# A recurrence and a feed-forward layer on one core: r loaded packed from chunk 2 on, its columns put in order by GpSimd, and q k^T for pairs of units

## The chip, the core and the metric

The kernel runs on one core of a Trainium2 chip. The core has five engines with a queue of instructions each: TensorE (PE, matrix products, with PEld for its weight loads), VectorE (DVE), ScalarE (ACT), GpSimd (POOL) and SyncE (SP, which issues transfers); transfers run on 16 DMA engines that all queues share. SBUF is the working memory of 128 partitions; PSUM, with eight banks of 128 x 512 fp32, takes the results of TensorE. The metric is the device time of one execution in microseconds (us), the median of several runs.

## What is computed

B = 4 batches, H = 8 heads, S = 768 tokens, D = 48. First a recurrence along the tokens with one decay `w` and one bonus `u` per head and channel, then a layer with a squared ReLU (384 to 2048 to 384) over all 3072 tokens:

```python
state = zeros(B, H, D, D)
for t in range(S):
    cur = einsum('bhd,bhe->bhde', u[None] * k[:, :, t], v[:, :, t])
    y[:, :, t] = einsum('bhd,bhde->bhe', r[:, :, t], state + cur)
    state = w[None, :, :, None] * state + einsum('bhd,bhe->bhde', k[:, :, t], v[:, :, t])
x = y.transpose(0, 2, 1, 3).reshape(B * S, H * D)
h = maximum(x @ moe_w_in, 0)
out = (h * h) @ moe_w_out
```

All inputs and the output are fp32 in HBM.

## The kernel before

The tokens are cut into six chunks of C = 128; a chunk of one batch is a unit, 24 units in all, unit i = (chunk i // 4, batch i % 4). Inside a unit the recurrence is turned into products: r is multiplied by powers of the decay (`wpos`), k by the inverse powers (`wneg`), and the masked product of the two replaces the loop over tokens. A state per batch carries over from chunk to chunk.

The steps of a unit are small functions:

- `load` brings r, k or v of a unit from HBM, token by token: a partition holds one token, 8 heads of 48 numbers. The units 2 to 5 load through GpSimd's queue, all others through SP's.
- `scale` (L296, instruction on L300, VectorE) multiplies r (x = 0) or k (x = 1) by its powers and writes bf16 into a padded buffer `rkw`, 64 columns a head; `NPAD` such buffers are used in turn.
- `turn` with `evict_rk` (units 0 to 5, TensorE and ScalarE) or `turn_dma` (L306, units 6 to 23, one transfer of SP that transposes) puts r and k with their channels on the partitions, in `rkT`: two heads stand on one set of 128 partitions, 64 rows each.
- `rk` (L326, VectorE) multiplies the two for the term with u. `at` (L331) is q k^T: eight matmuls of 64 rows by 128 columns, two of them (the two heads of a set) in the two halves of the array, into two PSUM banks. `mask` (L346, VectorE, twice a unit) takes a bank to bf16 in SBUF and cuts it to the causal triangle.
- `sums` (L351) makes the term with u and the unit's addition to the state, `diag_v` (L368), `state_add`, `state_decay` (VectorE) and `state_cast` (ScalarE) keep the state, `y_mm` (L393) forms y from the masked product, v and the state, `evict_y` (L412) adds the term with u, and `x_turn` with `evict_x` or `x_dma` (L423, a transfer of SP) transposes y.
- `mm1` (L437) is the first layer (one unit at a time, 12 matmuls of 128 columns a step, for the units 0 to 7; two units at a time, 6 matmuls of 256 columns a step, from unit 8 on), `relu` (ScalarE) and `square` (ScalarE or VectorE) its activation, `mm2` (L466, four matmuls of 384 columns a step) the second layer, `evict_o` (ScalarE) and `store` the way out, mostly through GpSimd's queue.
- `weights` loads a quarter of one weight matrix through GpSimd's queue. `fill` (L244) is a matmul on a constant tile whose result nobody reads.

Nothing but the text `SCHEDULE` sets the order. It is a list of words `step:arguments@banks`; the program goes through it once and calls the functions, and each engine does its instructions in the order in which they are called. A number and a star ahead of a word repeat it; the numbers behind @ are the PSUM banks that the step takes. So a step that is moved in the list is moved past all steps of its engine or queue between the two places. `room` says how many buffers each kind of tile has; an instruction that writes into a buffer waits until the earlier use of it is over.

```python
for word in SCHEDULE.split():
    times, _, word = word.rpartition("*")
    word, _, taken = word.partition("@")
    name, *args = word.split(":")
    given[:] = [int(x) for x in taken.split(",") if x]
    for _ in range(int(times or 1)):
        steps[name](*[value(x) for x in args])
```

`at_pair`, which calls `at` for a unit and for the next one, is in the file; the list before does not use it.

Of the kernel before, what the change touches and what calls it, by code (L numbers as in the profile page):

```python
# [17 lines left out]
load:0:kt fill@0 load:0:rt 2*fill load:1:rt 2*fill load:0:vt fill columns 2*fill spread_log@1 load:1:kt load:2:rt  # L18
load:1:vt weights:kt.0:0:I fill power:0 3*fill load:2:kt power:1 scale:0:0 load:9:kt 3*fill scale:0:1 turn:0:0@2
load:3:rt load:6:kt scale:1:0 fill evict_rk:0:0 fill turn:0:1@3 load:2:vt fill evict_rk:0:1 spread_columns@4  # L20
load:3:kt cast_v:0 rk:0 fill scale:2:0 at:0@5,6 copy_columns fill u_columns mask:0:1 turn:1:0@7 mask:0:0
evict_rk:1:0 weights:-:1:I sums:0@1 weights:-:2:I y_mm:0@2 diag_v:0 load:8:kt fill scale:1:1 2*fill load:3:vt fill
evict_y:0 3*fill scale:2:1 turn:1:1@3 weights:-:0:O 3*fill x_turn:0@4 turn:2:0@6 evict_x:0 fill scale:3:0
weights:-:3:I 2*fill evict_rk:1:1 4*fill evict_rk:2:0 fill rk:1 load:4:rt fill at:1@7,5 turn:2:1@2 mask:1:1
turn:3:0@4 load:5:rt evict_rk:2:1 3*fill mask:1:0 mm1:0:1:0@3 evict_rk:3:0 end_columns rk:2 fill relu:0:1:0 fill
scale:3:1 4*fill cast_v:2 fill load:6:rt at:2@6,5 cast_v:1 fill mask:2:1 4*fill turn:3:1@2 mask:2:0 sums:2@4
evict_rk:3:1 fill sums:1@7 load:4:kt diag_v:2 y_mm:1@3 y_mm:2@5 diag_v:1 mm1:0:1:1@6 weights:-:1:O evict_y:1 fill
relu:0:1:1 3*fill evict_y:2 load:4:vt 2*fill x_turn:1@2 state_add:1 evict_x:1 mm1:0:1:2@3 weights:-:2:O state_add:0
fill relu:0:1:2 fill mm1:1:1:0@6 cast_v:3 rk:3 x_turn:2@5 relu:1:1:0 state_add:2 at:3@2,7 evict_x:2 mm1:1:1:1@3
weights:-:3:O mask:3:1 square:0:1:0:1 sums:3@1 square:0:1:2:1 mask:3:0 mm1:2:1:0@6 load:7:kt square:1:1:0:1  # L30
square:0:1:1:0 mm2:0:0@4 state_cast:1 diag_v:3 y_mm:3@5 mm1:2:1:1@7 relu:2:1:0 evict_y:3 load:5:kt mm2:1:0@2
state_add:3 square:2:1:0:1 state_cast:0 x_turn:3@6 fill load:5:vt mm1:0:1:3@5 relu:1:1:1 mm1:2:1:2@1 scale:4:0
relu:2:1:1 mm1:2:1:3@3 evict_x:3 scale:5:0 fill relu:2:1:3 mm1:3:1:0@7 relu:2:1:2 mm1:1:1:3@6 scale:4:1
square:1:1:1:1 turn:4:0@3 relu:1:1:3 fill mm1:3:1:3@1 evict_rk:4:0 square:1:1:3:0 mm2:2:0@6 relu:3:1:0
square:2:1:1:0 relu:0:1:3 turn:4:1@3 fill square:2:1:3:0 mm1:3:1:1@7 evict_rk:4:1 relu:3:1:3 square:0:1:3:0 mm2:1:1
square:3:1:0:1 rk:4 mm2:0:1 relu:3:1:1 turn:5:0@5 square:2:1:2:1 at:4@3,1 state_cast:2 mm2:3:0@7 mask:4:0
square:3:1:1:1 mm2:0:2 mask:4:1 load:7:rt cast_v:4 mm2:2:1 evict_rk:5:0 sums:4@3 y_mm:4@1 diag_v:4 fill mm2:2:2
evict_y:4 mm2:2:3 scale:5:1 mm2:0:3 state_add:4 x_turn:4@5 load:8:rt turn:5:1@0 evict_x:4 scale:6:1 mm1:1:1:2@1
evict_rk:5:1 mm1:4:1:0@3 relu:1:1:2 rk:5 square:3:1:3:0 at:5@5,0 relu:4:1:0 mm1:4:1:1@1 scale:6:0 cast_v:5 mask:5:0
turn_dma:6 mm1:4:1:3@3 relu:4:1:1 mask:5:1 square:4:1:0:1 sums:5@5 mm2:3:1 diag_v:5 square:1:1:2:1 load:6:vt  # L40
square:4:1:1:0 evict_o:0 mm1:4:1:2@1 store:0:POOL scale:7:0 y_mm:5@0 relu:4:1:2 scale:7:1 mm2:1:2 relu:4:1:3
evict_y:5 turn_dma:7 mm2:1:3 state_cast:3 state_decay:4 square:4:1:3:0 x_turn:5@4 mm2:4:0@1 evict_x:5 scale:8:1
load:9:rt state_cast:4 mm2:4:1 state_add:5 load:7:vt evict_o:1 mm1:5:1:3@3 square:4:1:2:1 state_decay:5 load:10:rt
rk:6 mm1:5:1:0@0 relu:5:1:3 scale:9:1 cast_v:6 at:6@4,5 mm1:5:1:1@2 mask:6:1 mm2:4:2 scale:8:0 relu:5:1:1 rk:7
relu:5:1:0 turn_dma:8 mm2:4:3 mask:6:0 state_cast:5 sums:6@3 square:5:1:3:0 mm1:5:1:2@5 square:5:1:1:1 load:8:vt
diag_v:6 y_mm:6@2 relu:5:1:2 mm1:3:1:2@0 evict_y:6 square:5:1:0:1 at:7@4,5 square:5:1:2:1 x_dma:6 mm2:5:0@2 mask:7:1
relu:3:1:2 mm2:5:1 state_add:6 square:3:1:2:1 load:10:kt load:11:rt cast_v:7 mm2:5:2 scale:9:0 mask:7:0 mm2:3:2
turn_dma:9 scale:10:0 sums:7@0 y_mm:7@5 diag_v:7 mm2:5:3 cast_v:8 state_decay:6 evict_y:7 evict_o:4 at:8@3,4
state_cast:6 state_add:7 store:4:POOL mm2:3:3 x_dma:7 rk:8 mm1:6:1:0@1 store:1:POOL scale:10:1 load:9:vt mm1:6:1:1@5
relu:6:1:0 mask:8:1 load:11:kt mm1:6:1:3@0 mask:8:0 relu:6:1:1 square:6:1:0:1 sums:8@1 square:6:1:1:0 mm1:6:1:2@4  # L50
relu:6:1:3 state_add:8 mm2:6:0@5 relu:6:1:2 turn_dma:10 diag_v:8 evict_o:3 y_mm:8@3 square:6:1:2:1 mm2:6:1 evict_y:8
evict_o:5 state_decay:7 at:9@0,4 x_dma:8 rk:9 mm1:7:1:0@1 mask:9:0 mm1:7:1:1@7 square:6:1:3:0 load:10:vt cast_v:9
load:12:rt relu:7:1:0 mask:9:1 sums:9@3 evict_o:2 mm2:6:2 diag_v:9 square:7:1:0:1 store:2:POOL scale:11:0
mm1:7:1:3@2 relu:7:1:1 state_add:9 store:5:POOL y_mm:9@0 relu:7:1:3 mm1:7:1:2@1 evict_y:9 square:7:1:1:1 scale:11:1
at:10@4,6 x_dma:9 relu:7:1:2 state_decay:8 mm2:7:0@7 state_decay:9 square:7:1:2:1 rk:10 mm2:6:3 turn_dma:11
mask:10:1 mm2:7:1 evict_o:6 square:7:1:3:0 store:6:POOL mm2:7:2 cast_v:10 mask:10:0 load:12:kt state_cast:7
load:11:vt store:3:POOL mm2:7:3 scale:12:0 state_cast:8 sums:10@3 y_mm:10@2 diag_v:10 mm1:8:2:0@0 evict_y:10
mm1:8:2:1@1 x_dma:10 mm1:8:2:3@6 relu:8:2:1 state_cast:9 mm1:8:2:6@5 square:8:2:1:0 load:13:rt load:13:kt rk:11
at:11@4,2 relu:8:2:0 scale:12:1 mm1:8:2:4@1 relu:8:2:3 turn_dma:12 square:8:2:0:1 mm1:8:2:2@0 square:8:2:3:0
relu:8:2:4 mask:11:1 mm1:8:2:5@6 relu:8:2:2 load:12:vt mask:11:0 mm2:9:0@1 cast_v:11 load:14:rt square:8:2:4:1  # L60
state_add:10 mm1:8:2:7@2 square:8:2:2:1 sums:11@0 relu:8:2:6 y_mm:11@4 diag_v:11 mm2:8:0@3 relu:8:2:7 evict_y:11
relu:8:2:5 mm2:8:1 state_decay:10 x_dma:11 scale:13:1 square:8:2:5:1 mm2:9:1 scale:13:0 square:8:2:6:1 mm2:9:2
square:8:2:7:0 turn_dma:13 evict_o:7 at:12@5,2 rk:12 mm2:8:2 mask:12:0 load:13:vt cast_v:12 mm2:8:3 mask:12:1
load:14:kt mm2:9:3 load:15:rt sums:12@4 mm1:10:2:0@6 diag_v:12 load:15:kt y_mm:12@7 relu:10:2:0 mm1:10:2:1@5
evict_y:12 state_cast:10 rk:13 mm1:10:2:2@2 x_dma:12 state_add:11 relu:10:2:1 at:13@6,7 evict_o:9 square:10:2:1:0
# [51 lines left out]
def kernel(  # L117
# [13 lines left out]
    C = 128  # L131
# [14 lines left out]
    room = {'ldr': 3,  # L146
            'ldk': 8,
            'ldv': 4,
            'rkw': 4,
            'g': 2,  # L150
            'rkT': 3,
            'vb': 6,
# [405 lines left out]
```

## Time and profile before

| | us |
|---|---|
| median of 3 runs | 178.05 (177.88 to 178.28) |
| the profiled execution | 177.38 |
| its span, from the first to the last instruction | 175.6 |
| TensorE busy | 169.5 |
| VectorE busy | 130.0 |
| ScalarE busy | 128.3 |
| GpSimd busy | 32.6 |
| fills (L245), 68 of them, busy | 14.0 |
| `at` (L337), 192 matmuls, busy | 9.7 |
| loads of r through SP's queue, 20, from issue to landing (median) | 4.4 |
| transposes of `rkw` through SP's queue, 18, from issue to landing (median) | 3.8 |

The span starts at 0 with the first instruction; 1.8 us of the execution lie around it. A line of a group gives the source line, the engine, the operation, the tiles written and read with their shapes, how many there were, the busy time and the mean length of one, then the idle time of the engine ahead of them and what ended it. A matmul's length counts from its start to the end of its last result, so that matmuls that follow each other overlap in the record, and busy times of the lines of TensorE add up to more than the engine's. Slices cut the span into 40 equal parts, with the busy share of each in tenths.

### The profile page before, as it was taken

Reading aid. Unit: us, or ns where it says so; the run is one execution under the profiler, and the core shown is the slowest. Engines: PE = TensorE matmul, PEld = TensorE weight load, DVE = VectorE, ACT = ScalarE, POOL = GpSimd, SP = SyncE. Lnnn points to the kernel's source line nnn. Section 1 sums busy time; section 2 is a strip of 40 time slices with the busy share of each in tenths; the row PEclk is TensorE's granted clock in tenths of the full one; section 3 lists DMA queues with packets and bytes.
Section 4 is the critical chain, followed back from the end, with each engine's and each line's share of the span. In section 5 each row is a group of like instructions: output and inputs, shape, how many; then the busy total and the mean of one; then the engine's idle time right before and its main releaser. Section 6 shows DMA issues by size and latency. Waiting matters only on the chain.

```text
span 175.6 us, 4843 instructions
## 1 busy us (share of the span) xinstructions
PE 169.5 (97%) x1946; PEld 134.0 (76%) x1946; DVE 130.0 (74%) x280; ACT 128.3 (73%) x266; POOL 32.6 (19%) x66
## 2 busy tenths in 40 slices
PE   7999999999999999999999999999999999999990
PEld 3668889868777788787786896886895976879770
DVE  4486897658998999878699989889777598560400
ACT  4616599976889499599396797499497894895930
POOL 8987444000100202200020003000030300000020
PEclk9999999999999999999999999999999999999998
DMA  5999999994797998799899999978999996410023
GB/s 109 197 221 183 218 221 214 232 166 95 156 181 136 235 157 215 175 193 155 168 157 223 182 139 257 197 139 165 191 221 173 204 199 115 82 52 19 0 90 134
DMA packets 93848, 28.83 MB, mean 164 GB/s; under 512 B 89681, under 2 KB 91730, under 8 KB 93826
## 3 DMA queue, kind: packets, MB, share of 16 engines
q1 hardware_dynamic: 89472, 18.88, 62.1%
q0 software_dynamic: 4352, 9.64, 23.1%
q8 instruction: 15, 0.25, 0.6%
q14 instruction: 7, 0.06, 0.1%
q10 hardware_dynamic: 2, 0.00, 0.0%
HBM read 20.45 MB, written 4.72 MB: 143 GB/s over the span
## 4 chain that ended last, share of the span: by engine, by line
PE 94%; ACT 1%; DVE 1%; issue 1%; POOL 0%; ACTq 0%
PE bank L447 37%; PE bank L471 35%; PE bank L245 5%; PE bank L337 4%; PE bank L400 3%; PE bank L362 2%; PE bank L406 2%; PE bank L320 2%; PE bank L486 2%; PE bank L357 1%; PE bank L249 1%; PE bank L431 1%; ACT L190 0%; ACT rkT L324 0%; ACT lnw L209 0%
## 5 line engine op out<-in xcount | busy, mean ns | idle before, releaser
L447 PE MATMUL bank<-xT,w_in_q 128*128 128x128 bf16 (+1 forms) x768 | 70.8, 246 | 0.0
L471 PE MATMUL bank<-w_out_q,g 128*128 128x384 bf16 x368 | 67.4, 326 | 0.0
L447 PEld LDWEIGHTS <-w_in_q 128*128 128x128 bf16 x768 | 64.1, 114 | 2.3
L455 ACT ACTIVATE gr<-bank 128x512 f32<-128x512 f32 x96 | 54.3, 599 | 15.5 <-PE bank L447 14.7
L471 PEld LDWEIGHTS <-g 128*128 128x128 bf16 x368 | 33.7, 98 | 19.4 <-ACT g L462 0.5
L462 ACT ACTIVATE g<-gr 128x512 bf16<-128x512 f32 x60 | 36.2, 636 | 0.5
L505 POOL DMA_DIRECT2D out_dram<-osb x21 | 11.4, 545 | 128.4 <-ACT osb L478 127.9
L349 DVE TENSOR_TENSOR am<-bank,smask 128x512 bf16<-128x512 f32 x48 | 31.7, 686 | 3.2 <-PE bank L337 2.9
L464 DVE TENSOR_TENSOR g<-gr 128x512 bf16<-128x512 f32 x36 | 24.4, 686 | 12.8 <-ACT gr L455 12.8
L391 ACT CAST stb<-st 64x192 bf16<-64x192 f32 x40 | 13.9, 348 | 5.7 <-DVE st L385 5.4
L371 DVE TENSOR_TENSOR dv<-vb,bank 128x384 f32<-128x384 bf16 x24 | 13.2, 552 | 6.3 <-PE bank L362 4.7
L300 DVE TENSOR_TENSOR rkw<-ldr,wpos 128x384 bf16<-128x384 f32 x24 | 13.3, 553 | 3.6 <-ACT wpos L253 2.4
L415 DVE TENSOR_TENSOR yb<-bank,dv 128x384 bf16<-128x384 f32 x24 | 13.3, 556 | 2.7 <-PE bank L406 1.7
L245 PE MATMUL bank<-warm 128*128 128x256 bf16 x68 | 14.0, 335 | 1.2 <-DVE warm L193 1.2
L304 ACT CAST vb<-ldv 128x384 bf16<-128x384 f32 x24 | 12.3, 511 | 3.8 <-DMA ldv<-in_v_dram 3.7
L478 ACT COPY osb<-bank 128x384 f32<-128x384 f32 x23 | 10.9, 477 | 4.9 <-PE bank L471 4.9
L300 DVE TENSOR_TENSOR rkw<-ldk,wneg 128x384 bf16<-128x384 f32 x24 | 13.3, 553 | 0.9 <-DMA ldk<-in_k_dram 0.7
L329 DVE TENSOR_TENSOR rk<-rkT 128x512 bf16<-128x512 bf16 x24 | 10.1, 421 | 4.2 <-ACT rkT L324 2.6
L381 DVE TENSOR_TENSOR st<-bank,st 64x192 f32<-64x192 f32 x32 | 11.3, 352 | 0.9 <-PE bank L362 0.6
L245 PEld LDWEIGHTS <-warm 128*128 128x128 bf16 x68 | 7.2, 116 | 3.9 <-issue 1.3
L337 PE MATMUL bank<-rkT 64*128 64x128 bf16 x192 | 9.7, 222 | 0.0
L337 PEld LDWEIGHTS <-rkT 64*128 64x128 bf16 x192 | 5.5, 95 | 5.2 <-issue 3.2
(61 smaller groups left out, 118.0 us busy)
## 6 DMA issues: line engine op xcount, KB each, us to landing
out_dram<-osb POOLq DMA_DIRECT2D x21, 192.0 KB, 3.7
ldk<-in_k_dram SPq DMA_DIRECT2D x20, 192.0 KB, 4.5
ldr<-in_r_dram SPq DMA_DIRECT2D x20, 192.0 KB, 4.4
ldv<-in_v_dram SPq DMA_DIRECT2D x20, 192.0 KB, 4.0
w_in_q<-in_moe_w_in_dram POOLq DMA_DIRECT2D x4, 384.0 KB, 9.9
w_out_q<-in_moe_w_out_dram POOLq DMA_DIRECT2D x4, 384.0 KB, 11.7
ldr<-in_r_dram POOLq DMA_DIRECT2D x4, 192.0 KB, 10.5
ldk<-in_k_dram POOLq DMA_DIRECT2D x4, 192.0 KB, 9.1
```

The lines of the kernel that those rows point to most:

```text
L245: nc.tensor.matmul(out=bank("fill")[:, :WIDE], lhsT=warm[:, :128], rhs=warm, start=True, stop=True)
L300: nc.vector.tensor_tensor(t["rkw"][:, x, :, :, :D], pair(src), pair(wx), ALU.mult)
L337: nc.tensor.matmul(out=t["at"][o][:, p, :], lhsT=t["rkT"][sl, 1, p, :], rhs=t["rkT"][sl, 0, p, :], start=True, stop=True,)
L349: nc.vector.tensor_tensor(am, t["at"][o], smask.unsqueeze(1).to_broadcast([C, HP, C]), ALU.mult)
L371: nc.vector.tensor_tensor(t["dv"], t["vb"], t["d"].unsqueeze(2).to_broadcast([C, H, D]), ALU.mult)
L391: nc.scalar.copy(stb[b][sl, :, o * D : (o + 1) * D], st32[b][sl])
L415: nc.vector.tensor_tensor(t["yb"], t["y"], t["dv"].rearrange("p h d -> p (h d)"), ALU.add)
L447: nc.tensor.matmul(out=t["h", s][:, a], lhsT=turned, rhs=chunks[c]["xT"][:, n, b : b + m, :], start=(n == 0), stop=(n == NK - 1),)
L455: nc.scalar.activation(t["gr", s], t["h", s], AF.Relu)
L462: nc.scalar.activation(g, x, AF.Square)
L464: nc.vector.tensor_tensor(g, x, x, ALU.mult)
L471: nc.tensor.matmul(out=t["o"], lhsT=chunks[units[i][0]]["g"][:, f, units[i][1], :], rhs=w_out_q[f // 4][:, f % 4, :], start=(f == 0), stop ...
```

## The change

The units of the chunks 0 and 1 stay as they are. For the chunks 2 to 5, r is treated a chunk at a time:

- `load4` loads one batch of a chunk with four tokens on a partition (32 partitions, 8 heads, 4 x 48 numbers in one run), so that four loads fill the 128 partitions with the four batches.
- `scale4` multiplies two of the four token places of all four batches at once by powers of the decay that belong to this layout (`wpos4`, made by `power4` on ScalarE from a copy of the log, `keep_log`), `turn4` transposes them, in two halves each.
- In what comes out, the columns of a unit stand as (place of four, token of 32). `gather` copies them for one unit into the order of the tokens, on GpSimd, into one of three buffers `rTu`.
- k of two neighbouring units is scaled into one buffer (`scale_k`) and transposed by one transfer (`turn_k`).
- `at_pair` makes q k^T of both units one after the other, with four banks taken.

The numbers of loads and of transposing transfers stay (72 and 36), and the matmuls and fills do too. `packed_consts` prepares constants on GpSimd. Numbers of buffers change (`room`, `NPAD` 5), and the whole list is written anew: steps that the change does not name stand elsewhere too.

```diff
-    PAIRED = ()
+    PAIRED = (8, 10, 12, 14, 16, 18, 20, 22)
-    room = {'ldr': 3, ..., 'rkw': 4, 'rk': 3, 'am': 4, 'gr': 6, ...
+    room = {'ldr': 4, ..., 'rkw': 5, 'rk': 2, 'am': 9, 'gr': 8, ...
+            'ldr4': 1, 'rw4': 1, 'r4T': 2, 'kw2': 2, 'kT2': 2, 'rTu': 3}
...
+    def packed_consts():
+        time = const.tile([128, 1], mybir.dt.int32, name="time")
+        for b in range(B):
+            nc.gpsimd.iota(time[b * NP : (b + 1) * NP], pattern=[[0, 1]], base=0, channel_multiplier=J)
+        for j in range(J):
+            nc.gpsimd.tensor_scalar(up4[:, j : j + 1], time, 1.0, float(j - C // 2), ALU.mult, ALU.add)
+        for x in rw4_b + kw2_b:
+            nc.gpsimd.memset(x[:, :, :, :, D:], 0.0)
+    def keep_log():
+        nc.scalar.copy(lnb, spread["log"])
+    def power4(j):
+        nc.scalar.activation(wpos4[:, j].rearrange("p h d -> p (h d)"), lnb, AF.Exp, scale=up4[:, j : j + 1])
+    def load4(c, b):
...
+        nc.sync.dma_start(
+            out=chunks[c]["r4"][b * NP : (b + 1) * NP].rearrange("p h j d -> p h (j d)"),
+            in_=r[b, :, c * C : (c + 1) * C, :].rearrange("h (p j) d -> p h (j d)", j=J),
+        )
+    def scale4(c, n):
...
+        j = slice(2 * n, 2 * n + 2)
+        nc.vector.tensor_tensor(
+            x["rw"][:, j].rearrange("p j a o e -> p j (a o) e")[:, :, :, :D], x["r4"][:, :, j, :].rearrange("p h j d -> p j h d"),
+            wpos4[:, j], ALU.mult,
+        )
+    def turn4(c, n):
...
+        nc.sync.dma_start_transpose(
+            out=x["rT"][:, j].rearrange("p j a c -> p (j a) c"), in_=x["rw"][:, j].rearrange("p j a o e -> p (j a o e)"),
+        )
+    def gather(i):
+        c, b = units[i]
+        x = tiles[i]["rT"] = buffer("rTu", [128, HP, C], BF16)
+        e = nc.gpsimd if ('POOL', 1.0)[0] == "POOL" else nc.vector
+        e.tensor_copy(
+            x.rearrange("p a (q j) -> p a j q", j=J), chunks[c]["rT"][:, :, :, b * NP : (b + 1) * NP].rearrange("p j a q -> p a j q"),
+        )
+    def scale_k(i):
...
+        nc.vector.tensor_tensor(t["kw"][:, :, :, :D], pair(t["kt"]), pair(wneg), ALU.mult)
+    def turn_k(i):
+        x = buffer("kT2", [128, 2, HP, C], BF16)
+        nc.sync.dma_start_transpose(
+            out=x.rearrange("p n a c -> p (n a) c"), in_=pairs[i]["kw"].rearrange("p n a o e -> p (n a o e)"),
+        )
...
     def at(i):
...
-                    out=t["at"][o][:, p, :], lhsT=t["rkT"][sl, 1, p, :], rhs=t["rkT"][sl, 0, p, :],
+                    out=t["at"][o][:, p, :], lhsT=t["kT"][sl, p, :], rhs=t["rT"][sl, p, :],
```

`rk`, `sums` and `y_mm` read the new tiles in the same way. Some places of the list, before and after:

```diff
-load:0:kt fill@0 load:0:rt 2*fill load:1:rt 2*fill load:0:vt fill columns 2*fill spread_log@1 load:1:kt load:2:rt
-load:1:vt weights:kt.0:0:I fill power:0 3*fill load:2:kt power:1 scale:0:0 load:9:kt 3*fill scale:0:1 turn:0:0@2
...
-square:8:2:7:0 turn_dma:13 evict_o:7 at:12@5,2 rk:12 mm2:8:2 mask:12:0 load:13:vt cast_v:12 mm2:8:3 mask:12:1
-load:14:kt mm2:9:3 load:15:rt sums:12@4 mm1:10:2:0@6 diag_v:12 load:15:kt y_mm:12@7 relu:10:2:0 mm1:10:2:1@5
...
+load:1:rt fill@0 load:0:rt 2*fill load:0:kt 2*fill load:0:vt fill columns fill spread_log@1 load:1:kt load:3:rt
+load:1:vt load:2:rt fill power:0 fill weights:rt.1:0:I power:1 scale:0:0 load:6:kt spread_columns@2 scale:0:1
+load:2:kt turn:0:0@3 scale:1:0 turn:0:1@4 evict_rk:0:0 load:3:kt fill evict_rk:0:1 turn:1:0@5 load:2:vt rk:0 fill
...
+x_dma:8 state_decay:8 mm1:7:1:0@2 mask:9:0 relu:7:1:1 evict_o:5 mask:9:1 mm2:6:1 load4:3:1 relu:7:1:0 store:5:POOL
+scale_k:11 mm1:7:1:3@3 square:7:1:1:1 turn_k:10 square:7:1:0:1 sums:9@6 y_mm:9@7 diag_v:9 mm1:7:1:2@5 square:6:1:3:0
+load:10:vt mm2:6:2 relu:7:1:2 evict_y:9 relu:7:1:3 state_add:9 mm2:7:0@1 x_dma:9 square:7:1:2:1 fill square:7:1:3:0
+mm2:7:1 load:11:vt scale4:3:1 mm2:6:3 load:12:kt mm2:7:2 evict_o:6 scale4:3:0 state_cast:8 at_pair:10@2,5,7,3
...
+cast_v:12 gather:14 load:15:kt mm2:9:2 cast_v:13 load:14:kt mm2:9:3 load:14:vt rk:12 at_pair:12@5,7,2,6 evict_o:9
+load4:4:2 sums:12@1 load:15:vt mask:12:1 mm1:10:2:0@3 mask:12:0 mm1:10:2:2@4 relu:10:2:0 load4:4:3 diag_v:12
...
+square:14:2:7:0 mm2:15:0@1 relu:14:2:5 gather:19 diag_v:17 square:14:2:5:1 mm2:14:0@7 evict_y:17 store:12:POOL
+square:14:2:4:1 mm2:14:1 state_add:17 x_dma:17 relu:14:2:6 store:10:POOL at_pair:18@0,6,2,4 rk:18 square:14:2:6:1
```

More of the change, by code (lines that the diff above doesn't have):

```diff
@@ L23 @@
[L23 to L62, printed above, removed]
@@ L298, in scale @@
         t["rkw"] = rkw_b[i % NPAD]
+        t["kw"] = t["rkw"][:, 1]
         src, wx = (t["kt"], wneg) if x else (t["rt"], wpos)
```

201 lines of the change are left out of this document (135 added, 66 removed).

## The prediction

> **What bounds the kernel now.** I read the head of the page (busy times, 40 slices, the chain's share by engine), then the table of ten-microsecond windows, then the timeline of TensorE around one q k^T step, and last the rows for the engines that get new work.
>
> ```profile
> PE 169.5 (97%) x1946; PEld 134.0 (76%) x1946; DVE 130.0 (74%) x280; ACT 128.3 (73%) x266; POOL 32.6 (19%) x66
> PE   7999999999999999999999999999999999999990
> PE 94%; ACT 1%; DVE 1%; issue 1%; POOL 0%; ACTq 0%
> ```
>
> TensorE never rests, and the chain that ended last is TensorE for 94%. So time is gained only where TensorE's own list gets shorter, and lost only where something makes it wait. Busy TensorE is not TensorE at its pace, so I looked at where one group starts and the next one starts:
>
> ```profile
> 64.00 0.81 PE L471 MATMUL bank<-w_out_q,g 128*128 128x384 bf16 x4
> 64.75 0.40 PE L337 MATMUL bank<-rkT 64*128 64x128 bf16 x8
> 65.08 1.53 PE L447 MATMUL bank<-xT,w_in_q 128*128 128x128 bf16 x24
> 69.50 3.42 PE L471 MATMUL bank<-w_out_q,g 128*128 128x384 bf16 x20
> 72.76 0.24 PE L357 MATMUL bank<-uwb,rk 128*128 128x8 bf16 x4
> ```
>
> Columns: start, length, line. Twenty L471 start to start take 72.76 - 69.50 = 3.26, 0.163 each. So the four at 64.00 are through at 64.65, but `at` (L337, two half-height matmuls side by side) starts at 64.75 and the next step at 65.08. One `at` holds TensorE 65.08 - 64.65 = 0.43 us. Its four side-by-side pairs of 128 columns need 4 x 0.056 = 0.22 (0.67 us for the 12 matmuls of 128 columns in the chain of waits). **About 0.21 us of each `at` is the way into and out of the half-height form**, 24 times in the span.
>
> **The change, part by part.**
>
> *Pairs.* From unit 8 sixteen `at` become eight pairs of 16 half-height matmuls in a row: eight ways in and out fewer, 8 x 0.21 = 1.7 us. The other matmuls are the same in number and shape, fills too (68 before and after). If the second half must wait for its own operand, the gain is nothing: the bounds are 0 and 1.7. I take 1.7, since the operand of the second unit is listed well ahead (below).
>
> *Loads of r.* Sixteen loads of 1024 runs of 192 bytes become sixteen of 256 runs of 768 bytes, each into 32 partitions. Queue q1 spends 0.621 x 16 x 175.6 / 89472 = 19.5 ns on a packet of 211 bytes on average, q0 149 ns on one of 2215; 768 bytes lie at an estimated 56 ns. So 16384 x 19.5 - 4096 x 56 = 90 us over 16 engines, 5.7 us of DMA time saved. It buys nothing by itself: no DMA holds the chain. But one chunk's r is now whole only when four loads have landed, and the first half that `scale4` multiplies is then waited for on VectorE with masks and squares queued behind it. Words of the list go to each engine in order; the TensorE steps between two words are the time that the other engine has. From the last load of chunk 3 to its `scale4` these are two narrow mm1 (1.34), `sums` and `y_mm` (0.6), two or three mm2 (1.3 to 1.95): 3.3 to 3.9 us, against 4.4 us to landing for a load of r now and 1.7 for the smallest transfer in the trace. Chunk 2 has 6.4, chunks 4 and 5 have 4.6 and 5.2. A wait of 0 to 1.1 us once; 0.1 at the end, since VectorE has 10% to spare there.
>
> *VectorE.* `scale` of r goes 16 times at 0.553 (8.8 us); `scale4` comes 8 times at 0.95 (0.553 for 384 columns and 0.686 for 512 give 1.04 ns a column, 768 columns), 7.6 us. k is scaled as before. 1.2 us less on an engine that is off the path: nothing.
>
> *SP's queue.* 16 transposes become 8 `turn4` and 8 `turn_k` of the same 1024 columns, so the queue's length (1.2 to 1.9 us each) stays. `turn4` moves ahead of v loads and x transposes; from the second `turn4` of chunk 2 to the first pair stand 8.7 us of TensorE steps, against 3.8 to landing and two gathers.
>
> *GpSimd.* Sixteen gathers of 16 runs of 32, written with a step of 4: new to the trace. The nearest rows:
>
> ```profile
> masks.py:199 POOL TENSOR_SCALAR_AFFINE_SELECT identb<-identb 128x128 bf16<-128x128 bf16 x1 | 0.3, 294 | 0.1
> masks.py:199 POOL TENSOR_SCALAR_AFFINE_SELECT ident<-ident 4x4 f32<-4x4 f32 x1 | 0.2, 185 | 0.1
> masks.py:197 POOL MEMSET ident<- 4x4 f32 x1 | 0.1, 92 | 0.3 <-POOLq L542 0.3
> ```
>
> 124 more columns cost 109 ns, so 512 columns cost 185 + 508 x 0.88 = 0.63 us; that is the lower bound. If each of the 16 runs cost as much as the smallest instruction, 16 x 92 ns = 1.47 us is the upper one. I take 0.63, the row of the same form. 16 x 0.63 = 10 us on an engine that is busy 19%. A gather waits for its transpose and, with three buffers, for the `y_mm` three gathers back; behind it in the queue are stores of the output, for which four output buffers and the copies into them on ScalarE wait. The tightest is that of unit 19: it needs `y_mm` of 17, and three mm2 (1.95 us) later the pair 18/19 comes. Even 1.47 fits: nothing. `packed_consts` (four iota, four small arithmetic, three memsets, some 2.3 us from rows of 0.1 to 0.5) stands ahead of three loads of w_out, hidden in the waits of 1.9, 0.8 and 2.3 us that this queue has there now (on L455, a DMA, L371); 2.3 if they are gone.
>
> *ScalarE.* `keep_log` and four `power4` at 0.58 (row of L253) are 2.9 us in the first 50, where the windows show 15 us idle: nothing, and 2.9 if that cover were gone.
>
> *Masks.* A pair fills four of eight banks, and `y_mm` follows closer: after pair 12/13 come `sums` and two mm1, 1.6 us, where 2.9 stood between; two masks take 1.3. I add 0.3 for these places together (bounds 0 and three times 0.6).
>
> **Sum:** -1.7 + 0.1 + 0.3 = -1.3 us. The profiled execution took 177.38 us (span 175.6), so its like after is 176.1. The median of the runs is 178.05, 0.67 above the profiled one, so I forecast 178.05 - 1.3 = **176.7 us**.
>
> **Rivals.**
>
> *VectorE is held up by the gathers and becomes the bound (slower).* The windows, in columns of start:end, PE, PEld, DVE:
>
> ```profile
> 60.00:70.00 10.00, 10.00 (x170) 8.53 (x168) 9.76 (x22) 8.31 (x17) 1.08 (x2) 1.00 1.02 205
> 70.00:80.00 10.00, 10.00 (x104) 8.23 (x103) 8.18 (x17) 7.74 (x18) 1.08 (x2) 1.00 0.98 191
> 80.00:90.00 10.00, 10.00 (x117) 7.58 (x113) 8.00 (x17) 7.26 (x16) 0.00 (x0) 1.00 0.93 165
> 90.00:100.00 10.00, 9.97 (x107) 7.54 (x106) 9.71 (x23) 7.49 (x17) 1.08 (x2) 1.00 1.09 180
> 100.00:110.00 10.00, 10.00 (x109) 7.75 (x106) 9.19 (x19) 8.77 (x19) 1.63 (x3) 1.00 1.01 202
> ```
>
> VectorE is busy 44.8 of 50 us there, with 0.6 less after. If every gather stops it for its whole length, about eight gathers fit up to (50 - 44.2) / 8 = 0.72 us each; from there VectorE sets the pace and TensorE waits. At 1.05 us, half way between my bounds, it is 8 x 1.05 - 5.8 = 2.6 late; with further gathers in the remaining windows at 7 to 9 of 10 I add 0.4: 178.05 - 1.7 + 3.0 = **179.4**. For it: the two crowded windows. Against it: `scale` takes 548 to 560 ns in all 24 cases, also those beside GpSimd's DMA issues, so no stop shows so far; no GpSimd compute of such length runs beside VectorE in this trace. The Trainium skill, SBUF — State Buffer, section Who interferes with whom, speaks for it: a VectorE instruction with two SBUF inputs and a GpSimd instruction that reads SBUF exclude each other, and the later one waits for the whole of the first. By that rule only squares, `scale`, `rk` and the decay would stop, not masks and what reads a bank; no run here shows it yet.
>
> *The front gives part back.* Ahead of the first transpose stand 9 fills (15 before), ahead of the first mm2 55 (63 before), and the other 13 come later, the last near unit 7's mm2. If the front's data come no sooner, TensorE idles where 8 fills stood and pays them later: 8 x 0.11 = 0.9, **177.6**.
>
> *The clock is released later.* Seven fills from 10.88 take 0.21 us each, nine from 14.09 take 0.12:
>
> ```profile
> 10.15 0.25 PE L357 MATMUL bank<-uwb,rk 128*128 128x8 bf16 x4 [0.35 <-POOL uwb L267]
> 10.88 1.67 PE L245 MATMUL bank<-warm 128*128 128x256 bf16 x7
> 12.35 0.63 PE L320 MATMUL bank<-identb,rkw 128*128 128x128 bf16 x4
> 14.09 1.15 PE L245 MATMUL bank<-warm 128*128 128x256 bf16 x9
> 15.17 0.40 PE L337 MATMUL bank<-rkT 64*128 64x128 bf16 x8
> ```
>
> So TensorE goes at half pace until about 14.0, which is 3.9 us after the last idle piece (ended at 10.15). Fewer fills mean more idle; if one such piece moves the release by 3.9 us, half of it is lost: 178.05 - 1.7 + 1.9 = **178.25**, no change. The same skill's page TensorE: Matmul & The Clock Gate, Part 1, ties the release to free-running windows of about 3.4 us of sustained work; by that figure the loss would be 1.7. The trace agrees in kind (3.9 us without a gap).
>
> *The change does not do what it says:* the second `at` of each pair stands until its own gather is through, so the ways in and out are not saved but waited: 178.05 + 0.1 + 0.3 = **178.45**.
>
> **Numbers.** Forecast 0.50, VectorE 0.26, front 0.12, clock 0.08, no saving 0.04. What can be told from no change here is 0.2%, 0.36 us. Faster takes the forecast but 0.01 and 0.11 of the front: 0.60. Slower is VectorE: 0.26. The rest, 0.14, is the same. The forecast's own range is 175.2 (the front also shortens by its 8 fills, the small waits are not there, and 0.2 for the scatter of the runs: 178.05 - 1.7 - 0.9 - 0.2) to 177.4 (the small waits at half their upper bounds more); with the rivals 175.2 to 180.4, the upper end being VectorE at a gather of about 1.2 us.
>
> **What would show it.** Right: eight L337 groups of 16, each some 0.65 us from the end of the step before to the start of the next; TensorE idle nowhere after 20 us; gathers near 0.63. Wrong: groups that start late after a gather or a mask, `scale` or squares longer than 0.69 beside a gather, a DMA wait of some tenths before `scale4`, fills at 0.21 beyond 14 us.

## The result and the profile after

| | before | after |
|---|---|---|
| median | 178.03 us (177.88 to 178.28, 4 runs) | 183.06 us (182.11 to 184.24, 4 runs) |
| the profiled execution, its span | 177.38, 175.6 | 183.33, 181.6 |
| start of the last matmul in its trace | 170.9 | 176.8 |

The changed kernel is slower: ratio 1.0284, 95% interval 1.0221 to 1.0347. The forecast was 176.7 us with a range up to 180.4. A median here is taken over all runs of a kernel; a ratio is taken to the kernel before, timed beside it, and leaves out runs over 1.5% longer than the kernel's fastest.

First the head of the page of after and its groups on the engines that got new work (columns as in the tables before: busy us, mean ns of one, idle time before them and what ended it). In this kernel L303 is `gather`, L553 `square`, L438 `mask`, L316 `scale_k`, L320 `turn_k`, L426 `at`, L446 `sums`, L536 `mm1`, L560 `mm2`, L513 `x_dma`:

```profile
PE 168.1 (93%) x1946; PEld 133.2 (73%) x1946; DVE 136.7 (75%) x274; ACT 132.0 (73%) x271; POOL 56.8 (31%) x93
PE   6699999999999989999999799796999999999990
PE 32%; DMA 8%; DVE 8%; issue 0%; DVEq 0%; SPq 0%
...
L303 POOL COPY rTu<-r4T 128x512 bf16<-128x512 bf16 x16 | 22.6, 1465 | 57.1 <-DMA r4T<-rw 22.5
L553 DVE TENSOR_TENSOR g<-gr 128x512 bf16<-128x512 f32 x36 | 27.5, 776 | 13.3 <-ACT gr L544 13.1
L438 DVE TENSOR_TENSOR am<-bank,smask 128x512 bf16<-128x512 f32 x48 | 32.0, 685 | 2.6 <-PE bank L426 2.2
L316 DVE TENSOR_TENSOR kw<-ldk,wneg 128x384 bf16<-128x384 f32 x16 | 10.5, 660 | 0.1
```

TensorE, without a gap before, now has slices of 8, 7 and 6 tenths between 60 and 130 us (a slice is 4.5 us). The chain that ended last, followed back to 89.9 us, is now DMA and VectorE for a third of its length, where it was TensorE for 94% of the span. A gather takes 1.38 us at the median, 1.47 in the mean. VectorE has 1.2 us less to do by the change and is busy 6.7 us more: the square of 512 columns went from 686 to 776 ns, the scaling of k from 553 to 660, while the mask, which reads a bank, kept its 685. The waits of TensorE (us in total, times, longest):

```profile
PE bank L426 <- DMA kT<-kw: 2.4, 2, 1.4
PE bank L446 <- DVE rk L418: 1.4, 1, 1.4
...
PE bank L446 <- DVE am L438: 0.7, 1, 0.7
```

A pair in TensorE's timeline (start, length):

```profile
108.49 2.76 PE L560 MATMUL bank<-w_out_q,g 128*128 128x384 bf16 x16
111.19 0.62 PE L426 MATMUL bank<-rTu,kT 64*128 64x128 bf16 x16
111.74 1.47 PE L560 MATMUL bank<-w_out_q,g 128*128 128x384 bf16 x8
```

Sixteen L560 at 0.163 are through at 111.10, the next step starts at 111.74: a pair holds TensorE 0.64 us, where two single `at` held it 2 x 0.43. All eight pairs show it, two of them behind a wait.

**Where the time went.** Both lists of TensorE hold the same matmuls, so I took each matmul's start and subtracted the work listed before it at its own pace, fills left out. The difference between the two traces is then what was lost up to there. It is 0.2 us after the first 5 us of work, about 1.2 at 7, 1.3 at 40 and 5.9 at the end. After 40 us of work the pairs take off 1.6, so the waits that are new there are some 6.2 us: 1.3 at 63 us of the span, 1.1 at 100, 1.5 at 113, 0.3 at 117, 1.6 at 124, 0.4 at 152.

Three of them in the trace. At 63 and at 113 us, VectorE's and then GpSimd's timeline:

```profile
61.54 1.83 DVE L474 TENSOR_TENSOR st<-st,wend_c 128x192 f32<-128x192 f32 x1
63.40 0.69 DVE L438 TENSOR_TENSOR am<-bank,smask 128x512 bf16<-128x512 f32 x1
...
110.78 2.39 DVE L553 TENSOR_TENSOR g<-gr 128x512 bf16<-128x512 f32 x1
```

```profile
62.02 1.39 POOL L303 COPY rTu<-r4T 128x512 bf16<-128x512 bf16 x1
...
111.51 1.34 POOL L303 COPY rTu<-r4T 128x512 bf16<-128x512 bf16 x1
```

The state's decay, 0.35 us at the median, lasts until 63.37, where the gather ends at 63.41. Behind it in VectorE's queue is the mask, and `sums` on TensorE waits for that. The square at 110.78, 0.69 us elsewhere, lasts until 113.17; `rk` comes late behind it, and `sums` waits 1.4 us for `rk`. Both instructions start in the record 0.5 to 0.7 us ahead of the gather, while GpSimd issues a store, and without the gather would have been over by its start: why they were held that early is open (in e9 below, no instruction beside a store's issue is longer). At 100 us it is SP's queue:

```profile
92.47 2.31 SPq L513 DMA_TRANSPOSE xT<-yb  x1
94.83 0.57 SPq L275 DMA_DIRECT2D ldr<-in_r_dram  x1
95.45 0.45 SPq L364 DMA_DIRECT2D ldk<-in_k_dram  x1
96.01 2.25 SPq L320 DMA_TRANSPOSE kT<-kw  x1
```

k of units 14 and 15 is scaled at 94.17. SP issues an x transpose and two loads first, `turn_k` starts 1.8 us later and lands at 101.14, 5.1 us after its start (median 3.3), and the pair stands until then. At 124 it is the same: scaled at 118.29, the x transpose of unit 16 ahead, `turn_k` issued at 120.19 and landed 6.0 us later.

### The profile page after: what moved, and what is told of

It reads as the page before. It is cut to its first block, busy times and chain, and to the rows that moved or that the text cites. A ratio compares the mean times of both kernels' runs of the same rounds, so it can differ in the third digit from the quotient of the medians.

```text
span 181.6 us, 4885 instructions
## 1 busy us (share of the span) xinstructions
PE 168.1 (93%) x1946; PEld 133.2 (73%) x1946; DVE 136.7 (75%) x274; ACT 132.0 (73%) x271; POOL 56.8 (31%) x93
## 5 line engine op out<-in xcount | busy, mean ns | idle before, releaser
L536 PE MATMUL bank<-xT,w_in_q 128*128 128x128 bf16 (+1 forms) x768 | 71.5, 246 | 1.0 <-DMA w_in_q<-in_moe_w_in_dram 0.4
L536 PEld LDWEIGHTS <-w_in_q 128*128 128x128 bf16 x768 | 64.1, 113 | 4.5 <-DMA w_in_q<-in_moe_w_in_dram 0.9
L560 PE MATMUL bank<-w_out_q,g 128*128 128x384 bf16 x368 | 67.3, 326 | 0.0
L560 PEld LDWEIGHTS <-g 128*128 128x128 bf16 x368 | 34.1, 98 | 19.5 <-ACT g L551 0.4
L303 POOL COPY rTu<-r4T 128x512 bf16<-128x512 bf16 x16 | 22.6, 1465 | 57.1 <-DMA r4T<-rw 22.5
L553 DVE TENSOR_TENSOR g<-gr 128x512 bf16<-128x512 f32 x36 | 27.5, 776 | 13.3 <-ACT gr L544 13.1
L551 ACT ACTIVATE g<-gr 128x512 bf16<-128x512 f32 x60 | 36.9, 634 | 0.7
L438 DVE TENSOR_TENSOR am<-bank,smask 128x512 bf16<-128x512 f32 x48 | 32.0, 685 | 2.6 <-PE bank L426 2.2
L331 PE MATMUL bank<-warm 128*128 128x256 bf16 x68 | 15.2, 320 | 1.2 <-DVE warm L200 1.2
L567 ACT COPY osb<-bank 128x384 f32<-128x384 f32 x23 | 10.8, 480 | 5.1 <-PE bank L560 4.9
L413 ACT COPY rkT<-bank 128x512 bf16<-128x512 bf16 x12 | 6.7, 587 | 9.2 <-PE bank L409 9.2
L316 DVE TENSOR_TENSOR kw<-ldk,wneg 128x384 bf16<-128x384 f32 x16 | 10.5, 660 | 0.1
L331 PEld LDWEIGHTS <-warm 128*128 128x128 bf16 x68 | 6.7, 111 | 4.1 <-issue 1.3
L418 DVE TENSOR_TENSOR rk<-rTu,kT 128x512 bf16<-128x512 bf16 x16 | 7.7, 485 | 2.6 <-DMA kT<-kw 2.5
L489 PE MATMUL bank<-vb,am 128*128 128x48 bf16 x192 | 8.8, 183 | 0.0
```

The costliest lines, as they stand in the source:

```text
L303: e.tensor_copy(x.rearrange("p a (q j) -> p a j q", j=J), chunks[c]["rT"][:, :, :, b * NP : (b + 1) * NP].rearrange("p j a q -> p a j q"),)
L331: nc.tensor.matmul(out=bank("fill")[:, :WIDE], lhsT=warm[:, :128], rhs=warm, start=True, stop=True)
L438: nc.vector.tensor_tensor(am, t["at"][o], smask.unsqueeze(1).to_broadcast([C, HP, C]), ALU.mult)
L536: nc.tensor.matmul(out=t["h", s][:, a], lhsT=turned, rhs=chunks[c]["xT"][:, n, b : b + m, :], start=(n == 0), stop=(n == NK - 1),)
L551: nc.scalar.activation(g, x, AF.Square)
L553: nc.vector.tensor_tensor(g, x, x, ALU.mult)
```

## The experiments

Theory A: the gathers stop VectorE wherever it reads two operands from SBUF, and TensorE waits for what is late. Theory B: the k transposes are late by their place in SP's queue. The rivals were that only the gather's latency counts, that the new list loses time by itself, and, later, that the transfers in flight make the transposes late. The expectations call A the port theory.

### Set 1: the gather

**e1_unpacked**: the changed list with its pairs, but r loaded token by token and no gather.

```diff
-        nc.sync.dma_start(out=chunks[c]["r4"][b * NP : (b + 1) * NP]..., in_=r[b, ...].rearrange("h (p j) d -> p h (j d)", j=J))
+        nc.sync.dma_start(out=chunks[c]["r4"][:, b], in_=r[b, :, c * C : (c + 1) * C, :].rearrange("h s d -> s h d"))
...
+        tiles[i]["rT"] = chunks[c]["rT"][:, b]
```

> The same list with pairs, but r of chunks 2 to 5 is loaded token by token again (one batch into a quarter of the tile), multiplied by two instructions of 384 columns where one of 768 stood, and the gather is gone (its units read the transposed tile directly). Port theory (a gather takes GpSimd 1.47 us and stops VectorE's instructions with two SBUF inputs meanwhile, 8.0 us of VectorE in all, which is what TensorE waits for after 60 us): VectorE busy 136.7 - 8.0 - 7.5 + 8.8 = 130, TensorE's waits after 60 us fall from 6.3 to under 1.5, time 183.1 - 5 = 178. Latency theory (only the length of the gather on its own queue): the same, 178. List theory (pairs that take four banks, masks close behind, k transposes late in SP's queue): the waits stay, 181 or more.

185.01 us (183.38 to 186.96), ratio 1.0363 (1.0291 to 1.0435). VectorE went back to 130.3 us busy, with the square at 688 and the scaling of k at 553 ns. That is A's part of the trace. The time did not follow: its TensorE waits 4.1 us for `kT` and 2.2 for `xT`. So A alone does not explain the list; the edit also put 192-byte runs back, so it does not say what the gathers cost. (e9 below has the same list, no gathers either, and packed loads, and took 180.65.)

**e2_gather_act** and **e3_gather_dve**: the gather on ScalarE and on VectorE.

```diff
-        e.tensor_copy(
+        nc.scalar.copy(
...
-        e.tensor_copy(
+        nc.vector.tensor_copy(
```

> The gather is done by ScalarE in the same places of the list, 16 x 0.59 = 9.4 us more on an engine that is busy 132 of 182. Port theory: VectorE falls by 8.0 to 128.7, TensorE's waits after 60 us mostly go, some come back through a later ScalarE: 178.5 to 179.5. Latency theory: the same. List theory: 182 or more.

> The gather is done by VectorE in the same places of the list: 0.42 to 0.69 us each by the rows of 512 columns. Port theory: VectorE gets 6.7 to 11 us of copies in place of 8.0 us of stops, 136 to 140 busy, so TensorE waits much as in the changed kernel: 181.5 to 184. Latency theory: operands are ready 0.8 to 1 us sooner, 178 to 179.5. List theory: 183.

192.89 us (192.01 to 194.04), 1.084 (1.0774 to 1.0905), and 186.26 (184.18 to 188.26), 1.0424 (1.0349 to 1.05). VectorE's stretching is gone in e2 (129.5 us busy), but ScalarE is busy 149.2 us instead of 132.0, a gather taking it 1.35, and that costs more. On VectorE a gather takes 0.75 us and the engine comes to 138.3 us busy, about what the stops make of it on GpSimd (136.7). GpSimd is the least bad place for it in this list.

**e4_gather_twice**: each gather made a second time, into a spare tile.

```diff
+        for y in (gather_spare, x):
```

> Each gather copies twice on GpSimd, the first time into a tile that nobody reads: 2.9 us a unit in place of 1.47. Port theory: the stops double, VectorE 142 to 145 busy, 187 or more. Latency theory: only the gathers with little cover come later (units 9, 19, 16), 184 to 186, VectorE's own time as before. List theory: 183.

192.94 us (191.53 to 194.53), 1.0796 (1.0722 to 1.0869), VectorE 149.0 us busy, 12.3 more for 16 gathers more. Idle time on GpSimd would have hidden them; their stops on VectorE did not stay hidden. This speaks for A, though not alone: TensorE also waited 2.0 us for a gather itself, which is latency.

### Set 2: the k transposes earlier

**e5_unpacked_early** (from e1), **e6_packed_early** (from the changed kernel): from chunk 3 `scale_k` and `turn_k` one to three steps earlier, r loads 6 to 12 us earlier. **e7_packed_early_apart** is e6 with the pairs apart, **e8_packed_early_front** is e6 with the first 30 us in the order of before.

```diff
-... load4:4:1 scale_k:14 sums:13@5 load:16:kt relu:10:2:3 y_mm:13@4 scale_k:15 ... turn_k:14
+... mask:12:0 scale_k:14 ... scale_k:15 turn_k:14 load:15:vt mask:13:0 ... x_dma:12 ... load:16:kt
```

> Unpacked r as in the first experiment (185.01 us), and the order of the work changed in one respect: from chunk 3 the scalings and the transpose of k of each pair stand 1 to 3 us earlier, ahead of the x transpose and of the loads that stood directly before them, and the r loads of chunks 3 to 5 stand 6 to 12 us earlier. Theory 'k transposes late by their place in SP's order': TensorE's waits at the pairs of units 10, 14 and 18 (1.1, 1.6, 1.6 us) go and with them some of the 2.6 us that mm1 waited for x transposes: 178 to 180.5 us. Rival 'the loads token by token and the pair transposes do not fit in the time that is there, wherever they stand': the waits move, 184 to 186 us.

> The changed kernel (183.06 us) with the same new order, r packed and gathered on GpSimd. Theory 'two causes add: k transposes late by their place (1.04 + 1.5 us at the pairs of units 14 and 18), VectorE stopped beside gathers (1.3 + 1.5 + 0.3 us at 63, 113 and 117)': the first goes, the second stays, 180 to 181 us. Rival 'the gather alone': the k waits are only where time is spent that the gathers have already lost, so 182.5 to 183.5 us. Rival 'the list alone': all of the late waits go, 177.5 to 179 us.

> The run before this one with every pair of q k^T groups taken apart by one mm1 or mm2 step. Theory 'a pair saves one way into and out of half-height matmuls, 0.21 us, eight times': 1.7 us more than the run with pairs, 181.7 to 182.7 us if that takes 180.5. Rival 'the ways are hidden in other waits of TensorE': within 0.4 us of the run with pairs.

> The packed kernel in the new order, and its first 30 us (up to the transpose of unit 6) in the order of the kernel before, with the packed constants set in between. Theory 'the front's new order costs 1.0 to 1.3 us (fewer fills, a wait of 1.3 us for the w and u columns and of 0.5 us for w_in)': 179 to 179.8 us if the second run takes 180.5. Rival 'the front lost nothing that counts': within 0.4 us of the second run.

190.63 us (189.32 to 192.46), 193.8 (193.05 to 198.43), 194.22 (193.34 to 195.38) and 193.25 (193.11 to 194.59): all over 10 us above what the theory under test had named (e5 is 4.6 above its rival's range too). In e6 SP stood 16.7 us in total before `turn_k`, waiting for the scaled k, and the x transposes behind it in the same queue came late: TensorE waited 5.1 us for `xT` in four places, 2.6 for one `kT`. A transpose put ahead of its operand on an in-order queue holds everything behind it. e7 and e8 differ from e6 by less than its runs scatter; on an order that is held up by SP they say nothing on pairs or front. (In e8 one bank of the second product is written again before it is copied out; its work is that of e6.)

### Set 3: one cause at a time

**e9_no_gather**: the changed kernel, its list and loads, without gathers (a unit reads other tokens' columns, so the output is another; e12, e13, e14 and e17 do the same).

```diff
-        x = tiles[i]["rT"] = buffer("rTu", [128, HP, C], BF16)
...
+        tiles[i]["rT"] = chunks[c]["rT"][:, b]
```

> The changed kernel with its own order and the 16 gathers of GpSimd left out: a unit reads 128 columns of the transposed r as they lie, which are other tokens' (the output is another). Loads, scalings and transposes are as in the changed kernel. Theory 'VectorE is stopped beside the gathers, and that is 3.1 us of TensorE's late waits (1.3 at 63 us, 1.5 at 113, 0.3 at 117)': those go, the waits for k transposes (1.0 at 100 us, 1.5 at 124) stay, VectorE back to about 130 us busy: 179.5 to 180.5 us. Rival 'the gather counts only by its latency or not at all, the order of SP is all': 182 to 183.5 us. Rival 'all late waits come from VectorE running late behind the gathers, the k transposes too': 176.5 to 178 us.

180.65 us (179.88 to 181.18), ratio 1.0151 (1.0096 to 1.0206): 2.4 below the changed kernel. In its page the stretched rows are back at their old length, and the only late wait left is for k:

```profile
L549 DVE TENSOR_TENSOR g<-gr 128x512 bf16<-128x512 f32 x36 | 24.4, 687 | 13.6 <-ACT gr L540 13.2
L312 DVE TENSOR_TENSOR kw<-ldk,wneg 128x384 bf16<-128x384 f32 x16 | 8.7, 552 | 0.1
```

```profile
PE bank L422 <- DMA kT<-kw: 2.5, 3, 1.1
```

So the gathers cost 2.4 us here. The edit takes away both their stops and their latency; but in after's trace TensorE waits nowhere for a gather's result, while VectorE's stretched rows go with the gathers. So A holds; the median is 0.15 above what A named. What is left against before is the front and the waits for k. The last matmul starts at 173.37, 2.5 after that of before: -1.6 for the pairs, +1.3 in the front, +2.9 in three waits for k by the starts of its matmuls (1.0 at 73 us, 1.3 at 100, 0.6 at 123; the view of waits has 2.5), together 2.6.

e9 and e1 differ only in how r is loaded and scaled: 180.65 against 185.01. So in this list the packed loads are worth some 4.4 us, although the DMA engines are busy as long (1,112 and 1,118 us for the loads through SP). e1's waits for k and x transposes are longer (4.1 and 2.2 us against 2.5 and none over 0.15); why is not isolated.

**e10_front**: the first 30 us of the list in the order of before, the rest as in the changed kernel.

```diff
-load:1:rt fill@0 load:0:rt 2*fill load:0:kt ... spread_columns@2 scale:0:1
+load:0:kt fill@0 load:0:rt 2*fill load:1:rt ... turn_dma:6
```

> The changed kernel with its first 30 us (up to the transpose of unit 6) in the order of the kernel before, the packed constants set in between; everything behind in the changed kernel's order. Theory 'the front's order costs 1.0 to 1.3 us': 181.6 to 182.3 us. Rival 'what the front loses is made up later, or lost to the late waits whatever it does': 182.8 to 183.5 us.

184.87 us (183.16 to 184.99), 1.0356 (1.0294 to 1.0417). At 12 us of work its trace is 0.6 ahead of the changed kernel; at 40 it is 1.7 behind, since behind the joint of the two orders, between 30 and 47 us, TensorE waits 1.8 us in five places for ScalarE. It gives no price for the front: inconclusive.

**e11_swap**: three small moves on SP's queue, none ahead of its operand.

```diff
-... mm1:14:2:0@1 ... x_dma:16 ... turn_k:18
+... mm1:14:2:0@1 ... turn_k:18 x_dma:16
...
-... load:16:kt ... scale_k:15 ... turn_k:14
+... scale_k:15 ... turn_k:14 load:16:kt
```

(The third puts `load4:4:2` and `load4:4:3` behind `load:12:vt`.)

> The changed kernel with three small moves in SP's queue alone: the k transpose of units 18 and 19 ahead of the x transpose of unit 16 that waits for evict_y, one k load (unit 16) behind the k transpose of units 14 and 15 instead of ahead of it, and two r loads of chunk 4 some 7 us earlier, into a stretch in which SP waits. No step is put ahead of its operands, as the larger reordering of the second set did. Theory 'k transposes are late by what stands directly before them': the wait at the pair of units 14 and 15 goes (1.0 us), that at 18 and 19 shrinks from 1.5 us to under 0.5: 181 to 182 us. Rival 'they land late because of the transfers in flight, wherever they stand': 182.8 to 183.5 us. Rival 'what is put behind them is late instead, as in the larger reordering': over 184 us.

182.45 us (181.79 to 183.21), 1.0244 (1.0192 to 1.0295). In its trace the waits at 100 and 124 us are gone, as B says, and new ones of 0.7 and 0.5 us stand at 84 and 89, the latter for the next k transpose. The medians differ by 0.6 us with overlapping runs: the waits moved, and little was won.

**e12_all_three**: e9's, e10's and e11's edits in one kernel.

> The three edits together: gathers left out (other tokens of r are read, so the output is another), the front in the order of before, the three moves in SP's queue. If the parts add as the theories say (3.1 + 1.2 + 2.0 us below 183.06): 176.5 to 177.3 us, which is the predicted time. If something else is lost that no part covers: 178 us or more.

183.1 us (181.06 to 183.63), 1.0257 (1.0183 to 1.0332). The joint of e10 costs it 1.6 us by 40 us of work, so the sum of the parts was not tried cleanly here.

### Set 4: what was left

**e13_nog_swap**: e9 with e11's moves and the same for units 10 and 11. **e14_nog_swap_apart**: e13 with each pair taken apart.

```diff
-at_pair:12@5,7,2,6 evict_o:9 sums:12@1 mask:12:1 mm1:10:2:0@3
+at:12@5,7 evict_o:9 sums:12@1 mask:12:1 mm1:10:2:0@3 at:13@2,6
```

> Gathers left out (other tokens of r are read, so the output is another) and the small moves in SP's queue, with one more: the k transpose of units 10 and 11 ahead of the last r load of chunk 3, its scaling one mask earlier. Without gathers the kernel took 180.65 us and its trace shows 2.9 us of waits for k transposes (1.0 at 73 us, 1.3 at 100, 0.6 at 123). Theory 'they are late by their place in the queue': at least 2 of these go, 178 to 178.8 us. Rival 'the transfers need that long wherever they stand, or others are late instead': 180 to 181 us.

> The run before this one (gathers left out, so the output is another) with each pair of q k^T groups taken apart by one mm1 or mm2 step. Theory 'a pair saves one way into and out of half-height matmuls, 0.21 us, eight times': 1.7 us more than the run before. Rival 'it is hidden': within 0.4 us of it.

e13: 180.91 us (179.9 to 182.56), 1.0181 (1.011 to 1.0253), no better than e9. The k transposes at 100 and 123 came in time; x transposes, what hangs on them, and the k transposes of other pairs came late instead (1.0 us at 74, 0.5 at 75, 1.0 at 88, the last for the k of units 12 and 13):

```profile
PE bank L531 <- DMA xT<-yb: 1.2, 2, 0.8
...
PE bank L421 <- DMA kT<-kw: 1.0, 2, 0.8
```

So B in its simple form falls: these moves changed which transpose is late, and not how much is lost.

e14: 184.04 us (183.54 to 185.26), 1.0359 (1.0313 to 1.0405), 3.1 more than e13. In the two traces the last matmul is 3.6 apart. At 40 us of work e14 is 1.0 behind with the same list up to there, which is scatter. A pair holds TensorE 0.65 us from the step before to the step after, a single `at` in e14 0.43 unless something waits, so eight pairs save 8 x 0.2 = 1.6; the other 1.0 are later waits. The timeline shows a pair to be worth what was forecast; e14's time agrees in sign and can't be split more finely.

**e15_light**: in the front, the first w_in load ahead of unit 2's r load on GpSimd, the columns' transposes behind unit 0's, unit 6's k load later. **e16_swap_light**: these and the moves of e13, gathers kept.

```diff
-load:1:vt load:2:rt fill power:0 fill weights:rt.1:0:I power:1 scale:0:0 load:6:kt spread_columns@2 scale:0:1
+load:1:vt fill power:0 fill weights:rt.1:0:I load:2:rt power:1 scale:0:0 scale:0:1
```

> The changed kernel with three moves in its first 15 us alone: GpSimd issues the first w_in load before the r load of unit 2 instead of behind it, the transposes of the w and u columns stand behind those of unit 0, and the k load of unit 6 is issued later. Theory 'the front's 1.0 to 1.3 us are TensorE's waits for these transfers (1.26 us at 4.9, 0.5 us at 18.5)': 181.5 to 182.5 us. Rival 'the front is bound by all of the loads together, whatever comes first': 182.8 to 183.5 us.

> The changed kernel, gathers and full output kept, with the small moves in SP's queue and the three moves in the front. If both theories hold: 183.06 less 0.6 to 1.5 (queue) less 0.6 to 1.3 (front), 180.5 to 181.8 us; the gathers' 2.4 us stay, so it should not come below 180. If the moves only shift the waits: 182.5 us or more.

184.41 us (182.68 to 186.34), 1.0374 (1.0352 to 1.0396), and 186.31 (186.0 to 187.26), 1.0485 (1.0449 to 1.0522). The two waits aimed at are gone, but in e16's trace TensorE's transposes of the next units wait 1.8 us up to 13.6 and 0.7 up to 14.7. Behind these waits the granted clock is 0.51 from 16 to 19 us (1.00 in the changed kernel and in the kernel before), and the `at` at 16.16 holds TensorE 0.79 us, the one at 19.35 again 0.43. So the front loses the waits and then some 1.6 us more at half pace; at 40 us of work e16 is 2.1 behind the changed kernel. The step that was put first made another load late. No version tried beats the kernel before.

**e17_nog_vpool** (from e9) and **e18_vpool** (from the changed kernel): 16 v loads issued by GpSimd instead of SP.

```diff
-        (nc.gpsimd if i in (2, 3, 4, 5) else nc.sync).dma_start(
+        (nc.gpsimd if i in (2, 3, 4, 5) or (name == "vt" and i >= 8) else nc.sync).dma_start(
```

> Gathers left out (other tokens of r are read, so the output is another), the changed kernel's own order, and the 16 v loads of units 8 to 23 issued by GpSimd in place of SP, which has about 10 us less to issue. Without this the kernel took 180.65 us, with 2.9 us of waits for k transposes. Theory 'SP's queue is too full between 60 and 130 us': the waits shrink to under 1 us and the time to 178 to 179 us. Rival 'the transposes are late because VectorE's operands are, or because of the transfers in flight': 180 to 181.5 us.

> The changed kernel, gathers and full output kept, with the 16 v loads issued by GpSimd. Theory 'SP's queue is too full': the waits for k transposes (1.0 and 1.5 us) go, 181 to 182 us. Rival as for the run before: 182.8 to 183.5 us. If the v loads wait behind gathers and stores in GpSimd's queue, or GpSimd's own issuing stops VectorE: 184 us or more.

197.38 us (194.63 to 198.09), 1.1041 (1.0954 to 1.1128), and 194.49 (192.16 to 198.58), 1.093 (1.0887 to 1.0974). SP had 16 issues less and its transposes took longer, as its queue in e17 shows:

```profile
69.07 2.62 SPq L316 DMA_TRANSPOSE kT<-kw  x1
71.78 1.20 SPq L509 DMA_TRANSPOSE xT<-yb  x1
73.08 0.53 SPq L360 DMA_DIRECT2D ldk<-in_k_dram  x1
74.23 7.79 SPq L295 DMA_TRANSPOSE r4T<-rw  x1
```

Issuing that transpose takes 7.79 us, 1.4 at the median in the changed kernel; a k transpose takes up to 10.8 us to land. GpSimd issued four v loads in a row from 69 to 72.5 us. Between 71 and 75 us the records show 45 packets of 4,224 bytes from its queue of about 1.1 us each on the same DMA engines (0.3 at the median in the changed kernel), and the transposes' packets of 256 bytes between them. Fewer entries in SP's queue did not help: the third rival, the transfers in flight, is the one that this run speaks for; TensorE waits 11.1 us for k transposes in it, and the granted clock falls to 0.956 (0.998 in e9). How much of the changed kernel's own late landings (5.1 and 6.0 us) it explains was not isolated: before, a transpose also took up to 7.3 us to land, and no `at` started more than 0.2 us after the step ahead of it.

## Why the prediction was wrong

**GpSimd: "Even 1.47 fits: nothing" (the step that failed first).** The sum prices a gather by its length alone; what it does to VectorE is put at nothing there and left to a rival with a chance of 0.26. e9 shows 2.4 us for it. The length was wrong as well: "I take 0.63, the row of the same form" was 1.38 at the median and 1.47 in the mean, at the upper bound. Luck has a part in that bound: it priced each of the 16 runs, but ScalarE takes 1.35 us and VectorE 0.75 for the same copy, and no run here varied the number of runs. As to latency alone the "fits" was right: TensorE waits for no gather in after's trace.

**That rival's mechanism is what happened.** Of the scalings of k, squares, decays and `rk` of after, the records of 23 overlap a gather's, and 12 of these are over a tenth longer than elsewhere, 8.1 us together; of the masks, `dv`, `yb` and state additions, which read a bank, 18 overlap one and none is. The 12 end within 0.35 us of the end of a gather; of the other 11, six start ahead of the gather and five in its last 0.3 us. The Trainium skill, SBUF — State Buffer, section Who interferes with whom, says just this of VectorE with two SBUF inputs; the trace agrees in these counts, but for the two early starts above. Its price was not mine: (8 x 1.47 - 5.8) + 0.4 would be 6.4 us, e9 shows 2.4. It took every gather to stop VectorE for its whole length, 23.4 us in 16 gathers; the stops are 8.1 us, and most of these found slack.

**SP's queue (the second step that failed).** "16 transposes become 8 `turn4` and 8 `turn_k` of the same 1024 columns" is true and beside the point. The cover was worked out for `turn4` alone; from `turn_k` to its pair the list has 3.3 to 7.4 us of TensorE's steps, much as before (3.3 to 8.3). What I did not price is that `turn_k` is issued behind an x transpose and loads that have waits and landings of their own: 1.8 and 1.9 us from the scaled k to its issue, then 5.1 and 6.0 to landing, against 5.9 and 5.2 us of steps. In e9 the waits for k are 2.9 us. e11 and e13 show that they can be moved to other transposes; no run removed them, so why the landings are late stays open.

**The front.** The rival "gives part back" had 0.9 us and a chance of 0.12; 1.3 were lost by 40 us of work, most of it by the first 7. Five traces with this front (after, e9, e11, e13, e14) lose 1.3, 1.3, 1.9, 0.5 and 1.4, so the loss is there and scatters. Where it goes is open: e10 and e15 did not separate it. The clock is no part of it in after: its fills start 0.11 us apart from 13.8 us on, against 14.1 before. The rival of the clock did come in e16, behind a wait of 1.8 us.

**The pairs** were right: 0.2 us each in the timeline, eight times.

**The small terms.** For the load of r, 0.1 was set for a wait of VectorE; the profile has 1.2 us before one `scale4`, whose part in the end was not isolated. "5.7 us of DMA time saved" was none by the DMA engines' busy time (last section), yet "It buys nothing by itself" does not fit e1 and e9, 4.4 us apart. For masks 0.3 was set; the one wait for a mask (0.7) is that behind the stopped decay.

**The sum redone:** 178.0 - 1.6 (pairs) + 1.3 (front) + 2.9 (k transposes in e9) = 180.6, where e9 has 180.65, and + 2.4 (gathers) = 183.0, where 183.06 was measured. Neither sum is a test: the front and the waits for k are read off e9's own trace, and the 2.4 is the difference of the two runs. They show that the account has no large gap. Shown by an experiment are the gathers' 2.4; the front's 1.3 and the k transposes' 2.9 are located in the traces and not fully explained.

## What to carry to other kernels

A copy that only reorders costs its own length and what it stops on the other engine, at the places where that engine's queue has no slack; an engine that is idle 80% of the time is not free. On an in-order DMA queue count, for each transpose that something waits for, what stands ahead of it, when its operand is ready and the longest landing in the trace, not the queue's length; moving it ahead of its operand made all behind it late (e6). Where a list is tight, undo the causes one by one: two edits that each took away a wait, e11 and e13, brought others.

## What the runs showed of the hardware

- A GpSimd copy of 128x512 bf16 in 16 runs of 32, written with a step of 4, took 1.34 to 1.87 us, median 1.38; on ScalarE it took 1.35 us (e2), on VectorE 0.75 (e3). In after's trace two long ones, 1.63 and 1.87, begin while VectorE's square is under way, so there the gather seems to be the one held up.
- Longer packets did not shorten the DMA engines' work: before, 61,440 packets of 192 bytes held them 1,088 us, 17.7 ns each; after, 45,056 held them 861, 19.1 each, and 4,096 of 768 bytes 247, 60 each, so 1,108 in all.
- Transposes from SP came late beside loads that GpSimd issues: with 16 v loads moved there (e17) a transpose's issue took up to 7.8 us and its landing up to 10.8.
- The same list has a front that scatters: up to 20 us the waits of TensorE are 3.5 us in e13's trace and 4.6 in e14's.
- Behind waits of TensorE of 1.8 and 0.7 us (e16) the granted clock was 0.51 for some 3 us; behind one of 1.4 us in e14's front it stayed at 1.00.
